# Gated linear attention, capacity routing and two expert layers on one core: attention matmuls grouped by tiling mode, weight conversion in place in one PSUM bank

## The chip, the cores and the metric

One core of one Trainium2 chip. The time is device microseconds (us) of one execution; less is better. A core has five engines that run beside each other: TensorE (PE, with its weight loads listed as PEld), VectorE (DVE), ScalarE (ACT), GpSimd (POOL) and SyncE (SP, which here issues DMA). Each takes its instructions in the order in which they were written.

## The reference, cut to what matters

```python
# attention: B, H, S, D = 4, 8, 768, 48
f = 1 / (1 + exp(-f_logit))
for t in range(S):
    state = f[:, :, t, :, None] * state + einsum('bhd,bhe->bhde', k[:, :, t], v[:, :, t])
    y[:, :, t] = einsum('bhd,bhde->bhe', q[:, :, t], state)
...
# x = y as (3072, 384); each of 8 experts takes at most 384 tokens, best logits first
h = maximum(x[mask] @ w1[e], 0); out[mask] = h @ w2[e]
...
# second layer for all tokens; w_in (384, 2048) and w_out (2048, 384) come as float64
h = x @ w_in
out = (h * cos(h)) @ w_out
```

## The kernel before, in words

The kernel has three stages: attention with the expert logits, a search for the first expert's tokens (`search`, `route`), and the experts with the cosine layer (`experts`). The change is in the first stage alone, which ends when the last logits are counted.

Attention runs in chunks of 128 tokens. A unit u is one chunk c of one batch b (c, b = divmod(u, 4), 24 units); p runs over four pairs of heads. Step i of the loop at the end of `attention` works on up to five units at once: loads of unit i+2; `forget` and `decay` of unit i (logs of the gates on ACT; their running sums A on PE); `scale` of unit i-1 (em, ep on ACT; kT, qT on POOL); `turn`, `scores` and `cut` of unit i-2 (k transposed; q times k into sc; masked by DVE into m); `mix` and `outer` of unit i-3 (y from the state and from m; kv as k times v); `carry`, `fade` and `gate` of unit i-4 (state plus kv on DVE, state times decay on POOL, the product xl that holds x and the logits on PE, copied by ACT into xx and summed by DVE into lg). After every fourth unit (every second at the end) `first_counts` picks each token's best expert on DVE (L189 to L196) and counts with a matmul (cn). All engines follow the order of this code, which `in_order` pins.

Beside this, the two matrices of the cosine layer are converted from float64 to a high and a low fp32r part by `resident_weights`: 28 pieces, 12 of w_in (128 x 512) and 16 of w_out (128 x 384). A piece takes an absolute value on ACT (`head`), four DVE operations on its bits, a copy to the high part on ACT, and a subtraction to the low part on DVE (`tail`). It is a generator, conv; `fill(n)` runs it to its n-th next stop. Before, a piece has seven stops, a step runs eight (fills of 3, 2 and 3) and the steps from 24 on run three more. The work tile `wv` lies in SBUF, two of them, and the absolute value of piece i+1 is issued ahead of piece i's DVE work; only the last value `w` lies in a PSUM bank.

An fp32 matmul stands in the trace as two passes, each with its own weight load. Tiling modes: A, xl, tk and the state part of y use all 128 rows and columns of the array; y from m and kv use 128 rows and 48 columns; sc uses 64 rows.

Of the kernel before, what the change touches and what calls it, by code (L numbers as in the profile page):

```python
# [9 lines left out]
F32 = mybir.dt.float32  # L10
F32R = mybir.dt.float32r
BF16 = mybir.dt.bfloat16
I32 = mybir.dt.int32
AF = mybir.ActivationFunctionType
ALU = mybir.AluOpType
# [4 lines left out]
P = 128  # L20
B, H, S, D = 4, 8, 768, 48
# [3 lines left out]
NP = H // 2  # L25
# [5 lines left out]
TINY = 2.0**-15  # L31
# [71 lines left out]
def resident_weights(nc, wp, stg, ps, win, wout):  # L103
    V = nc.vector
    R = {
        "ih": wp.tile([P, 3, F2], F32R, name="wih"), "il": wp.tile([P, 3, F2], F32R, name="wil"),
        "oh": wp.tile([P, 16, HD], F32R, name="woh"), "ol": wp.tile([P, 16, HD], F32R, name="wol"),
    }
    wide = win.dtype != F32
    parts = []  # L110
    for k in range(3):
        for j in range(4):
            s = slice(j * 512, (j + 1) * 512)
            parts.append((R["ih"][:, k, s], R["il"][:, k, s], win[k * P:(k + 1) * P, s], 512))
    for f in range(16):
        parts.append((R["oh"][:, f], R["ol"][:, f], wout[f * P:(f + 1) * P, :], HD))
    raw, mid, fin = {}, {}, {}

    def load(i):
        if i < len(parts):  # L120
            n = parts[i][3]
            if wide:
                raw[i] = stg.tile([P, n, 2], I32, name="wr", tag="wr", bufs=3)
                nc.sync.dma_start(raw[i].rearrange("p n w -> p (n w)"), parts[i][2].bitcast(I32))
            else:
                raw[i] = stg.tile([P, n], F32, name="wr", tag="wr", bufs=3)
                nc.sync.dma_start(raw[i], parts[i][2])

    def head(i):
        if wide and i < len(parts):  # L130
            mid[i] = stg.tile([P, parts[i][3]], I32, name="wv", tag="wv", bufs=2)
            nc.scalar.activation(mid[i].bitcast(F32), raw[i][:, :, 1].bitcast(F32), AF.Abs)

    def tail(i):
        if i >= 0:
            V.tensor_tensor(parts[i][1], fin.pop(i), parts[i][0].bitcast(F32), op=ALU.subtract)

    def run():
        load(0)
        load(1)  # L140
        yield
        head(0)
        yield
        for i, (hi_part, _, _, n) in enumerate(parts):
            load(i + 2)
            head(i + 1)
            yield
            if wide:
                v, lo, hi = mid.pop(i), raw[i][:, :, 0], raw[i][:, :, 1]
                V.tensor_scalar(v.bitcast(F32), v.bitcast(F32), TINY, None, op0=ALU.max)  # L150
                yield
                V.tensor_scalar(v, v, 5, 2, op0=ALU.logical_shift_left, op1=ALU.logical_shift_right)
                yield
                V.scalar_tensor_tensor(v, hi, -2**30, v, op0=ALU.bitwise_and, op1=ALU.bitwise_or)
                yield
                tail(i - 1)
                yield
                fin[i] = ps.tile([P, n], F32, name="w", tag="w")
                V.scalar_tensor_tensor(fin[i].bitcast(I32), lo, 29, v, op0=ALU.logical_shift_right, op1=ALU.bitwise_or)
                yield  # L160
            else:
                tail(i - 1)
                fin[i] = raw[i]
                yield
            del raw[i]
            nc.scalar.copy(hi_part, fin[i])
            yield
        yield
        tail(len(parts) - 1)
    return R, run()  # L170


# [46 lines left out]
def attention(tc, nc, ctx, K, qk, qkvf, xs, Z, G, wp, wg, win, wout, consts, late):  # L219
    V, SC, PE, GP = nc.vector, nc.scalar, nc.tensor, nc.gpsimd  # L220
    ap = ctx.enter_context(tc.tile_pool(name="at", bufs=1))
    wk = ctx.enter_context(tc.tile_pool(name="wk", bufs=2))
    ps = ctx.enter_context(tc.tile_pool(name="aps", bufs=1, space=PSUM))
# [8 lines left out]
    yps = ps.tile([P, NP, P], F32, name="y", tag="y")  # L232
# [5 lines left out]
    st = {}  # L238

    def load(u):  # L240
        if u < NU:
            c, b = divmod(u, B)
            x = ring[u % 3]
            vf = wk.tile([P, 2, HD], F32, name="vf", tag="vf", bufs=6)
            src = qkvf[b, c * P:(c + 1) * P, 2:4]
            if u == 0:
                nc.sync.dma_start(vf[:, 1], src[:, 1])
            else:
                nc.sync.dma_start(vf, src)
            for j in range(2):  # L250
                nc.sync.dma_start(x[64 * j:64 * j + D], qk[b, c, j])
            if u == 0:
                nc.sync.dma_start(vf[:, 0], src[:, 0])
            st[u] = dict(x=x, v=vf[:, 0].rearrange("t (h d) -> t h d", h=H), f=vf[:, 1])
# [46 lines left out]
    def mix(u):  # L301
        c, b = divmod(u, B)
        d = st[u]
        T, v = st_all[b], d["v"]
        y = yps
        for p in range(NP):
            if c > 0:
                PE.matmul(y[:, p], T[:, p], d["qT"][:, p], start=True, stop=False)
            for j in range(2):
                PE.matmul(y[64 * j:64 * j + D, p], v[:, 2 * p + j], d["sc"][j][:, p], start=(c == 0), stop=True)  # L310
        yT = d["yT"] = wk.tile([P, NP, P], F32, name="yT", tag="yT")
        SC.copy(yT, y)

    def outer(u):
        if u // B < NCH - 1:
# [25 lines left out]
    def gate(u):  # L341
        c, b = divmod(u, B)
        yT = st.pop(u)["yT"]
        xl = ps.tile([P, NP, 2 * D + E], F32, name="xl", tag="tr")
        for p in range(NP):
            PE.matmul(xl[:, p], yT[:, p], K["turn"][:, p], start=True, stop=True)
        xx = wk.tile([P, HD], F32, name="xx", tag="xx", bufs=3)


        def rows():  # L350
            SC.copy(xx.rearrange("t (p e) -> t p e", p=NP), xl[:, :, :2 * D])
            nc.sync.dma_start(xs[b * S + c * P:b * S + (c + 1) * P], xx)

        if u < NU - 1:
            rows()
        yield
        V.tensor_reduce(Z["lg"][:, u], xl[:, :, 2 * D:].rearrange("t p e -> t e p"), axis=AX, op=ALU.add)
        if u == NU - 1:
            rows()
        yield  # L360
        n = B if c < NCH - 1 else 2
        if b % n == n - 1:
            yield from first_counts(nc, wk, ps, K, Z, u - n + 1, n)

    def warm_up(n):
        w = ps.tile([P, 512], F32, name="wp", tag="kv")
        for _ in range(n):
            PE.matmul(w, warm[:, :P], warm, start=True, stop=True)

    def turning():  # L370
        K["turn"] = ap.tile([P, NP, 2 * D + E], F32, name="turn")
        V.memset(K["turn"], 0.0)
        for j in range(2):
            r = slice(64 * j, 64 * j + D)
            for p in range(NP):
                V.tensor_copy(K["turn"][r, p, D * j:D * j + D], K["ident"][r, r])
            nc.sync.dma_start(K["turn"][r, :, 2 * D:], wg.rearrange("(p j e) x -> j e p x", p=NP, j=2)[j])

    R, conv = resident_weights(nc, wp, wk, ps, win, wout)
    load(0)  # L380
    load(1)
    nc.sync.dma_start(K["wg"], wg.rearrange("(k p) e -> p k e", p=P))
    next(conv)
    gates = iter(())
    tail = late(ps)
    for i in range(NU + 5):
        def at(k, f, *a):
            if 0 <= i - k < NU:
                f(i - k, *a)

        def fill(n):
            for _ in range(n):
                next(conv, None)
        counts, gates = gates, gate(i - 4) if 0 <= i - 4 < NU else iter(())
        if i > NU:
            next(tail, None)
        at(4, carry)
        next(gates, None)
        at(2, turn)
        at(1, scale)  # L400
        F = (3, 2, 3) if i > 1 else (0, 0, 0)
        fill(F[0])
        at(3, mix)
        at(0, forget)
        next(counts, None)
        next(gates, None)
        fill(F[1])
        at(2, scores)
        fill(F[2])
        at(2, cut, 0)  # L410
        at(2, cut, 1)
        next(gates, None)
        at(4, fade)
        at(3, outer)
        at(0, decay)
        fill(0 if i < NU else 3)
        if i < len(WARM) and WARM[i]:
            warm_up(WARM[i])
        if i == 0:
            turning()  # L420
        load(i + 2)
# [436 lines left out]
def kernel(ctx, tc, qk, qkvf, wg, wcat, win, wout, out):  # L858
# [33 lines left out]
    with ExitStack() as actx:  # L892
        with in_order(tc, nc):
            R = attention(tc, nc, actx, K, qk, qkvf, xs, Z, G, wp, wg, win, wout, consts, late)
# [55 lines left out]
```

## Time and profile before

| what | value |
|---|---|
| median of 3 runs | 883.29 us (883.09 to 887.6) |
| the profiled execution: its time, its span | 883.84 us, 882.1 us |
| attention with its counts, from the span's start | to 188.8 us |
| PE, DVE, ACT, POOL busy over the span | 93%, 70%, 41%, 45% |
| mean granted TensorE clock | 0.977 of full speed |

The span is the time from the first to the last instruction; 1.74 us lie around it. A share of busy time is a mean over stages with different limits, so the prediction reads the first stage alone. Everything after 188.8 us follows in one chain that the change does not touch.

### The profile page before, as it was taken

To read this page: it belongs to the slowest core of one execution; us is meant where nothing else is said; L and a number is where in the kernel's file an instruction comes from. 1 tells how busy PE (TensorE), PEld (TensorE's weight loads), DVE (VectorE), ACT (ScalarE), POOL (GpSimd) and SP (SyncE) were. 2 spreads that over 40 slices of the span, in tenths; PEclk is the share of its full clock that TensorE was granted. 3 is DMA by queue.
4 is the path that set the end of the run, shared out by engine and by line. 5 is a ranking of instruction groups with operands and counts; after the bars stand their busy time and mean duration, and the time that the engine had idled before them with its cause. 6 is when DMAs were issued, how large, how long until landed. Compare 5 with 4: busy or idle time off the path is not lost.

```text
span 882.1 us, 15725 instructions
## 1 busy us (share of the span) xinstructions
PE 824.7 (93%) x5866; PEld 757.0 (86%) x5866; DVE 615.7 (70%) x1495; ACT 363.8 (41%) x686; POOL 393.5 (45%) x326
## 2 busy tenths in 40 slices
PE   6889999953999999999999999999999999999996
PEld 4767777642899989998999899899989999999996
DVE  6999999975679558846974696479557845652553
ACT  4866666511333523342344135323523352533332
POOL 4655555402514732572366047513731474734233
PEclk9999999975899999999999999999999999999999
DMA  9876756302302300230113012201400233300000
GB/s 238 254 230 185 228 184 211 97 29 84 90 1 70 102 27 1 81 110 8 54 46 100 1 55 81 63 1 59 113 28 1 81 99 99 87 3 28 1 1 27
DMA packets 27348, 71.90 MB, mean 82 GB/s; under 512 B 4608, under 2 KB 7936, under 8 KB 27264
## 3 DMA queue, kind: packets, MB, share of 16 engines
q1 hardware_dynamic: 24192, 61.38, 23.6%
q0 software_dynamic: 3072, 9.44, 3.3%
q8 instruction: 48, 0.79, 0.4%
q14 instruction: 36, 0.29, 0.1%
HBM read 61.37 MB, written 9.44 MB: 80 GB/s over the span
## 4 chain that ended last, share of the span: by engine, by line
PE 68%; DVE 6%; issue 1%; POOL 1%; DMA 1%; POOLq 0%; ACT 0%; DVEq 0%
PE pC L703 8%; PE accD L766 8%; PE pC L704 7%; PE accD L768 7%; PE pC L705 7%; PE accD L767 7%; PE pA L703 4%; PE pA L704 3%; PE accB L703 3%; PE pA L705 3%; PE accB L704 3%; PE accB L705 3%; DVE C L513 1%; PE cn L509 1%; DVE thr L561 1%; DVE thr L553 1%
## 5 line engine op out<-in xcount | busy, mean ns | idle before, releaser
L756 POOL TENSOR_TENSOR gl<-g,gh 128x384 fp32r<-128x384 f32 x128 | 134.6, 1052 | 266.0 <-ACT gh L755 262.3
L686 POOL TENSOR_TENSOR wl<-raw,wh 128x768 fp32r<-128x768 f32 x64 | 118.4, 1856 | 40.7 <-ACT wh L685 40.1
L766 PE MATMUL accD<-woh,gh 128*128 128x384 f32 x384 | 131.0, 341 | 0.0
L768 PE MATMUL accD<-woh,gl 128*128 128x384 f32 x384 | 130.3, 339 | 0.5 <-POOL gl L756 0.5
L705 PE MATMUL pC<-yTh,wil 128*128 128x384 f32 x384 | 130.2, 339 | 0.0
L767 PE MATMUL accD<-wol,gh 128*128 128x384 f32 x384 | 129.4, 337 | 0.0
L704 PE MATMUL pC<-yTl,wih 128*128 128x384 f32 x384 | 129.4, 337 | 0.0
L703 PE MATMUL pC<-yTh,wih 128*128 128x384 f32 x384 | 129.0, 338 | 0.0
L750 ACT ACTIVATE fr<-fr,halfpi 128x384 f32<-128x384 f32 x128 | 78.8, 616 | 105.0 <-DVE fr L749 97.1
L752 DVE TENSOR_TENSOR g<-pC,fr 128x384 f32<-128x384 f32 x128 | 71.0, 555 | 62.7 <-ACT fr L750 61.1
L755 ACT CAST gh<-g 128x384 fp32r<-128x384 f32 x128 | 65.7, 514 | 111.7 <-DVE g L752 98.5
L747 DVE TENSOR_SCALAR ki<-pC 128x384 int32<-128x384 f32 x128 | 70.9, 554 | 19.8 <-PE pC L705 18.8
L695 DVE SCALAR_TENSOR_TENSOR hl<-pA,hh 128x384 fp32r<-128x384 f32 x64 | 35.5, 555 | 66.9 <-ACT hh L694 66.7
L685 ACT CAST wh<-raw 128x768 fp32r<-128x768 f32 x64 | 52.7, 834 | 64.0 <-PE accB L704 32.8
L694 ACT ACTIVATE hh<-pA 128x384 fp32r<-128x384 f32 x64 | 31.5, 492 | 112.4 <-PE pA L705 112.4
L768 PEld LDWEIGHTS accD<-woh,gl 128*128 128x128 f32 x384 | 72.1, 188 | 1.6 <-POOL gl L756 1.1
L749 DVE SCALAR_TENSOR_TENSOR fr<-pC,ki 128x384 f32<-128x384 f32 x128 | 71.1, 556 | 3.1
L704 PEld LDWEIGHTS pC<-yTl,wih 128*128 128x128 f32 x384 | 72.1, 188 | 0.5 <-DVE yTl L698 0.5
L766 PEld LDWEIGHTS accD<-woh,gh 128*128 128x128 f32 x384 | 72.2, 188 | 0.1
L767 PEld LDWEIGHTS accD<-wol,gh 128*128 128x128 f32 x384 | 72.2, 188 | 0.0
L705 PEld LDWEIGHTS pC<-yTh,wil 128*128 128x128 f32 x384 | 72.1, 188 | 0.1
L703 PEld LDWEIGHTS pC<-yTh,wih 128*128 128x128 f32 x384 | 72.0, 188 | 0.1
(178 smaller groups left out, 1745.4 us busy)
## 6 DMA issues: line engine op xcount, KB each, us to landing
raw<-in_wcat_dram SPq DMA_DIRECT2D x64, 384.0 KB, 3.4
ring<-in_qk_dram SPq DMA_DIRECT2D x48, 192.0 KB, 4.9
vf<-in_qkvf_dram SPq DMA_DIRECT2D x23, 384.0 KB, 5.5
wr<-in_win_dram SPq DMA_DIRECT2D x12, 512.0 KB, 5.6
wr<-in_wout_dram SPq DMA_DIRECT2D x16, 384.0 KB, 3.2
xs<-xx SPq DMA_DIRECT2D x24, 192.0 KB, 2.4
vf<-in_qkvf_dram SPq DMA_DIRECT2D x2, 192.0 KB, 3.4
xg<-xs,idx POOLq DMA_INDIRECT x24, 3.1
```

Of the source, the lines that this page charges most:

```text
L686: GP.tensor_tensor(l, raw, h.bitcast(F32), op=ALU.subtract)
L703: PE.matmul(o, ah, bh, start=first, stop=False)
L704: PE.matmul(o, ah, bl, start=False, stop=False)
L705: PE.matmul(o, al, bh, start=False, stop=last)
L747: V.tensor_scalar(ki, p, INV2PI, 0.25, op0=ALU.mult, op1=ALU.add)
L749: V.scalar_tensor_tensor(fr, p, INV2PI, ki, op0=ALU.mult, op1=ALU.subtract)
L750: SC.activation(fr, fr, AF.Sin, bias=halfpi, scale=TWO_PI)
L752: V.tensor_tensor(g, p, fr, op=ALU.mult)
L756: GP.tensor_tensor(gl, g, gh.bitcast(F32), op=ALU.subtract)
L766: PE.matmul(r["accD"][t], gh[:, s], R["oh"][:, f], start=(f == 0), stop=False)
L767: PE.matmul(r["accD"][t], gh[:, s], R["ol"][:, f], start=False, stop=False)
L768: PE.matmul(r["accD"][t], gl[:, s], R["oh"][:, f], start=False, stop=(f == NF - 1))
```

## The change

In `resident_weights` the SBUF tile `wv` is gone. ACT writes the absolute value into the PSUM bank `w`, the four DVE operations work on it in place, ACT copies it to the high part, DVE subtracts. The next piece's absolute value has to wait for that subtraction, since there is one bank. A piece has four stops, a step runs four (one at each fill), and the steps from 24 on run three more.

In `attention` the state part of y is issued for all four pairs first and y from m after it, `outer` (kv) directly behind, then `scores`, then `decay`. On ACT `scale` comes first in a step and the copy of y (`settle`) last.

```diff
-    def head(i):
-        if wide and i < len(parts):
-            mid[i] = stg.tile([P, parts[i][3]], I32, name="wv", tag="wv", bufs=2)
-            nc.scalar.activation(mid[i].bitcast(F32), raw[i][:, :, 1].bitcast(F32), AF.Abs)
-
-    def tail(i):
-        if i >= 0:
-            V.tensor_tensor(parts[i][1], fin.pop(i), parts[i][0].bitcast(F32), op=ALU.subtract)
...
-        for i, (hi_part, _, _, n) in enumerate(parts):
+        for i, (hi_part, lo_part, _, n) in enumerate(parts):
             load(i + 2)
-            head(i + 1)
-            yield
             if wide:
-                v, lo, hi = mid.pop(i), raw[i][:, :, 0], raw[i][:, :, 1]
-                V.tensor_scalar(v.bitcast(F32), v.bitcast(F32), TINY, None, op0=ALU.max)
+                lo, hi = raw[i][:, :, 0], raw[i][:, :, 1]
+                w = ps.tile([P, n], F32, name="w", tag="w")
+                v = w.bitcast(I32)
+                nc.scalar.activation(w, hi.bitcast(F32), AF.Abs)
                 yield
+                V.tensor_scalar(w, w, TINY, None, op0=ALU.max)
                 V.tensor_scalar(v, v, 5, 2, op0=ALU.logical_shift_left, op1=ALU.logical_shift_right)
                 yield
                 V.scalar_tensor_tensor(v, hi, -2**30, v, op0=ALU.bitwise_and, op1=ALU.bitwise_or)
-                yield
-                tail(i - 1)
-                yield
-                fin[i] = ps.tile([P, n], F32, name="w", tag="w")
-                V.scalar_tensor_tensor(fin[i].bitcast(I32), lo, 29, v, op0=ALU.logical_shift_right, op1=ALU.bitwise_or)
-                yield
+                V.scalar_tensor_tensor(v, lo, 29, v, op0=ALU.logical_shift_right, op1=ALU.bitwise_or)
...
+            nc.scalar.copy(hi_part, w)
+            yield
+            V.tensor_tensor(lo_part, w, hi_part.bitcast(F32), op=ALU.subtract)
             del raw[i]
-            nc.scalar.copy(hi_part, fin[i])
             yield
...
+        for p in range(NP) if c > 0 else ():
+            PE.matmul(y[:, p], T[:, p], d["qT"][:, p], start=(p == 0), stop=False, skip_group_check=True)
         for p in range(NP):
-            if c > 0:
-                PE.matmul(y[:, p], T[:, p], d["qT"][:, p], start=True, stop=False)
             for j in range(2):
-                PE.matmul(y[64 * j:64 * j + D, p], v[:, 2 * p + j], d["sc"][j][:, p], start=(c == 0), stop=True)
-        yT = d["yT"] = wk.tile([P, NP, P], F32, name="yT", tag="yT")
-        SC.copy(yT, y)
+                PE.matmul(y[64 * j:64 * j + D, p], v[:, 2 * p + j], d["sc"][j][:, p], start=(c == 0 and p == 0), stop=True, skip_group_check=True)
+
+    def settle(u):
+        yT = st[u]["yT"] = wk.tile([P, NP, P], F32, name="yT", tag="yT")
+        SC.copy(yT, yps)
...
+        F = int(i > 1)
+        at(1, scale)
         at(4, carry)
+        fill(F)
         next(gates, None)
         at(2, turn)
-        at(1, scale)
-        F = (3, 2, 3) if i > 1 else (0, 0, 0)
-        fill(F[0])
+        next(counts, None)
         at(3, mix)
+        at(3, outer)
         at(0, forget)
-        next(counts, None)
+        fill(F)
         next(gates, None)
-        fill(F[1])
+        fill(F)
+        at(3, settle)
         at(2, scores)
-        fill(F[2])
+        next(gates, None)
+        at(4, fade)
+        at(0, decay)
+        fill(F)
         at(2, cut, 0)
         at(2, cut, 1)
-        next(gates, None)
-        at(4, fade)
-        at(3, outer)
-        at(0, decay)
         fill(0 if i < NU else 3)
```

On PE, one step of a unit with c > 0, before; a row counts matmuls (xN) before they are split into passes:

```order
L346 MATMUL xl<-turn,yT 128x104 x4
L283 MATMUL tk<-ident,kT 128x128 x4
L308 MATMUL y<-qT,st_139 128x128
L310 MATMUL y<-m,vf 48x128 x2
L308 MATMUL y<-qT,st_139 128x128
L310 MATMUL y<-m,vf 48x128 x2
...
L294 MATMUL sc_1244<-qT,kT 128x128
L294 MATMUL sc_1245<-qT,kT 128x128
...
L321 MATMUL kv<-vf,kk 48x48 x8
L264 MATMUL A<-mask,logs_93 128x128 x4
```

The same step of the changed kernel (L291 and L294 are now the two parts of y, L278 sc, L307 kv, L248 A):

```order
L332 MATMUL xl<-turn,yT 128x104 x4
L267 MATMUL tk<-ident,kT 128x128 x4
L291 MATMUL y<-qT,st_139 128x128 x4
L294 MATMUL y<-m,vf 48x128 x8
L307 MATMUL kv<-vf,kk 48x48 x8
L278 MATMUL sc_1224<-qT,kT 128x128
L278 MATMUL sc_1225<-qT,kT 128x128
...
L248 MATMUL A<-mask,logs_93 128x128 x4
```

The two parts of y no longer alternate, and kv moved ahead of sc.

On DVE, one settled step before, from the sum of the logits on (m is the cut, st the carry, the rest conversion):

```order
L357 TENSOR_REDUCE lg<-xl 128x8
L150 TENSOR_SCALAR wv<-wv 128x384
L152 TENSOR_SCALAR wv<-wv 128x384
L154 SCALAR_TENSOR_TENSOR wv<-wr,wv 128x384
L298 TENSOR_TENSOR m<-sc_1244,mask 128x512
L298 TENSOR_TENSOR m<-sc_1245,mask 128x512
L331 TENSOR_TENSOR st_139<-st_139,kv 48x4x48 x2
L136 TENSOR_TENSOR wol<-w,woh 128x384
L159 SCALAR_TENSOR_TENSOR w<-wr,wv 128x384
```

The same place of the changed kernel (L141 to L145 work on the PSUM bank, L151 is the subtraction, L282 the cut, L317 the carry):

```order
L343 TENSOR_REDUCE lg<-xl 128x8
L144 SCALAR_TENSOR_TENSOR w<-wr,w 128x512
L145 SCALAR_TENSOR_TENSOR w<-wr,w 128x512
L151 TENSOR_TENSOR wil<-w,wih 128x512
L282 TENSOR_TENSOR m<-sc_1224,mask 128x512
L282 TENSOR_TENSOR m<-sc_1225,mask 128x512
L317 TENSOR_TENSOR st_139<-st_139,kv 48x4x48 x2
L141 TENSOR_SCALAR w<-w 128x384
L142 TENSOR_SCALAR w<-w 128x384
```

The subtraction of a piece now stands directly behind its fourth DVE operation, with ACT's copy between the two.

On DVE at the end of the stage, before (the last subtraction, the last two units' logits, the count):

```order
L159 SCALAR_TENSOR_TENSOR w<-wr,wv 128x384
L887 CAST flag<-tot 1x1
L136 TENSOR_TENSOR wol<-w,woh 128x384
L215 TENSOR_TENSOR cn<-cn,cn_2333 128x8
L357 TENSOR_REDUCE lg<-xl 128x8
L889 TENSOR_LOAD flag
L357 TENSOR_REDUCE lg<-xl 128x8
L189 TENSOR_REDUCE mx<-lg 128x2
...
L196 TENSOR_TENSOR oh<-w,wm 128x16
L215 TENSOR_TENSOR cn<-cn,cn_2369 128x8
L524 TENSOR_SCALAR sat<-cn 128x8
```

The same place of the changed kernel:

```order
L145 SCALAR_TENSOR_TENSOR w<-wr,w 128x384
L151 TENSOR_TENSOR wol<-w,woh 128x384
L877 TENSOR_LOAD flag
L141 TENSOR_SCALAR w<-w 128x384
L142 TENSOR_SCALAR w<-w 128x384
L144 SCALAR_TENSOR_TENSOR w<-wr,w 128x384
L145 SCALAR_TENSOR_TENSOR w<-wr,w 128x384
L343 TENSOR_REDUCE lg<-xl 128x8
L151 TENSOR_TENSOR wol<-w,woh 128x384
L173 TENSOR_REDUCE mx<-lg 128x2
...
L199 TENSOR_TENSOR cn<-cn,cn_2341 128x8
```

The last piece is now converted between the last two sums of logits. After step 23 six pieces are still to be subtracted, where it was four.

## Rows read from the trace of the kernel before

**Rows 1.** Busy time by stretch: start:end, length, then busy us and instructions.

```profile
core 0: us, PE busy (x) PEld busy (x) DVE busy (x) ACT busy (x) POOL busy (x), PEclk, DMA share, GB/s
...
60.00:80.00 20.00, 19.66 (x205) 15.28 (x205) 19.49 (x33) 13.49 (x29) 10.95 (x8) 1.00 0.72 218
```

**Rows 2.** Timeline (start us, length us): A of units 2, 9, 13, 23; last count.

```profile
16.84 1.16 PE L264 MATMUL A<-mask,logs 128*128 128x128 f32 x8 [2.79 <-ACT logs L259]
...
66.82 1.16 PE L264 MATMUL A<-mask,logs 128*128 128x128 f32 x8 [0.17 <-ACT logs L259]
...
95.39 1.16 PE L264 MATMUL A<-mask,logs 128*128 128x128 f32 x8 [0.17 <-ACT logs L259]
...
167.59 1.16 PE L264 MATMUL A<-mask,logs 128*128 128x128 f32 x8 [0.66 <-ACT logs L259]
...
188.66 0.16 DVE L215 TENSOR_TENSOR cn<-cn,cn 128x8 f32<-128x8 f32 x1 [0.28 <-PE cn L211]
```

**Rows 3.** Timeline, weight loads of PE in one step; in brackets idle time before.

```profile
88.20 0.97 PEld L264 LDWEIGHTS A<-mask,logs 128*128 128x128 f32 x8
89.09 0.97 PEld L346 LDWEIGHTS xl<-turn,yT 128*128 128x128 f32 x8
89.96 0.47 PEld L283 LDWEIGHTS tk<-ident,kT 128*128 128x128 f32 x4
90.40 0.30 PEld L308 LDWEIGHTS y<-qT,st 128*128 128x128 f32 x2
...
92.02 0.30 PEld L308 LDWEIGHTS y<-qT,st 128*128 128x128 f32 x2 [0.18 <-issue]
...
92.79 0.30 PEld L308 LDWEIGHTS y<-qT,st 128*128 128x128 f32 x2 [0.18 <-issue]
...
93.57 0.97 PEld L294 LDWEIGHTS sc<-qT,kT 64*128 64x128 f32 x16 [0.18 <-issue]
94.66 0.44 PEld L321 LDWEIGHTS kv<-vf,kk 128*48 128x48 f32 x16
...
95.39 0.97 PEld L264 LDWEIGHTS A<-mask,logs 128*128 128x128 f32 x8 [0.29 <-ACT logs L259]
```

**Rows 4.** The same view in a step of a unit with c = 0.

```profile
27.26 0.82 PEld L310 LDWEIGHTS y<-m,vf 128*48 128x48 f32 x16 [0.17 <-issue]
...
28.27 0.97 PEld L294 LDWEIGHTS sc<-qT,kT 64*128 64x128 f32 x16 [0.19 <-issue]
```

**Rows 5.** Instructions by line: ns min/median/max, first and last start us, forms.

```profile
L150 DVE TENSOR_SCALAR wv<-wv x28: 348/1068/1504, 15.2 to 179.2; 128x384 f32<-128x384 f32 x16, 128x512 f32<-128x512 f32 x12
...
L154 DVE SCALAR_TENSOR_TENSOR wv<-wr,wv x28: 550/692/1644, 17.1 to 180.0; 128x384 int32<-128x384 int32 x16, 128x512 int32<-128x512 int32 x12
...
L136 DVE TENSOR_TENSOR wol<-w,woh x16: 544/550/559, 98.4 to 184.4; 128x384 fp32r<-128x384 f32 x16
L136 DVE TENSOR_TENSOR wil<-w,wih x12: 679/684/692, 21.2 to 92.1; 128x512 fp32r<-128x512 f32 x12
...
L747 DVE TENSOR_SCALAR ki<-pC x128: 542/555/560, 254.9 to 868.2; 128x384 int32<-128x384 f32 x128
...
L132 ACT ACTIVATE wv<-wr x28: 531/596/714, 14.5 to 175.9; 128x384 f32<-128x384 f32 x16, 128x512 f32<-128x512 f32 x12
...
L166 ACT CAST wih<-w x12: 566/586/617, 18.6 to 88.3; 128x512 fp32r<-128x512 f32 x12
```

**Rows 6.** Timeline of DVE and ACT: expert choice, cut and carry, the last piece.

```profile
81.97 0.17 DVE L189 TENSOR_REDUCE mx<-lg 128x4 f32<-128x32 f32 x1
...
83.33 0.19 DVE L196 TENSOR_TENSOR oh<-w,wm 128x32 bf16<-128x32 f32 x1
...
161.76 1.28 DVE L298 TENSOR_TENSOR m<-sc,mask 128x512 f32<-128x512 f32 x2
...
162.96 0.71 DVE L331 TENSOR_TENSOR st<-st,kv 48x192 f32<-48x192 f32 x2
...
183.86 0.48 ACT L166 CAST woh<-w 128x384 fp32r<-128x384 f32 x1 [3.64 <-DVE flag L887]
...
184.37 0.56 DVE L136 TENSOR_TENSOR wol<-w,woh 128x384 fp32r<-128x384 f32 x1 [0.50 <-ACT woh L166]
```

More of the change, by code (lines that the diff above doesn't have):

```diff
@@ L116, in resident_weights @@
         parts.append((R["oh"][:, f], R["ol"][:, f], wout[f * P:(f + 1) * P, :], HD))
-    raw, mid, fin = {}, {}, {}
+    raw = {}
     def load(i):
@@ L141, in run @@
         yield
-        head(0)
-        yield
-        for i, (hi_part, _, _, n) in enumerate(parts):
+        for i, (hi_part, lo_part, _, n) in enumerate(parts):
             load(i + 2)
-            head(i + 1)
-            yield
             if wide:
-                v, lo, hi = mid.pop(i), raw[i][:, :, 0], raw[i][:, :, 1]
-                V.tensor_scalar(v.bitcast(F32), v.bitcast(F32), TINY, None, op0=ALU.max)
+                lo, hi = raw[i][:, :, 0], raw[i][:, :, 1]
+                w = ps.tile([P, n], F32, name="w", tag="w")
+                v = w.bitcast(I32)
+                nc.scalar.activation(w, hi.bitcast(F32), AF.Abs)
                 yield
+                V.tensor_scalar(w, w, TINY, None, op0=ALU.max)
                 V.tensor_scalar(v, v, 5, 2, op0=ALU.logical_shift_left, op1=ALU.logical_shift_right)
@@ L154, in run @@
                 V.scalar_tensor_tensor(v, hi, -2**30, v, op0=ALU.bitwise_and, op1=ALU.bitwise_or)
+                V.scalar_tensor_tensor(v, lo, 29, v, op0=ALU.logical_shift_right, op1=ALU.bitwise_or)
+            else:
+                w = raw[i]
                 yield
-                tail(i - 1)
-                yield
-                fin[i] = ps.tile([P, n], F32, name="w", tag="w")
-                V.scalar_tensor_tensor(fin[i].bitcast(I32), lo, 29, v, op0=ALU.logical_shift_right, op1=ALU.bitwise_or)
-                yield
[L161 to L164, printed above, removed]
+            nc.scalar.copy(hi_part, w)
+            yield
+            V.tensor_tensor(lo_part, w, hi_part.bitcast(F32), op=ALU.subtract)
             del raw[i]
-            nc.scalar.copy(hi_part, fin[i])
             yield
-        yield
-        tail(len(parts) - 1)
     return R, run()
```

## The prediction

> **What bounds the kernel now.** I read the busy times by stretch first, since the change is in the first stage alone. There PE is busy 19.66 of 20 us and DVE 19.49 of 20, ScalarE 13.49, POOL 10.95 [rows 1]: two engines are full at once, and easing one of them alone would show the other. Then the starts of A, one in each step: from unit 2 to unit 23 they take 167.59 - 16.84 = 150.75 us, and the last 14 steps (100.77 us) 7.20 us each [rows 2]. The stage ends at 188.82 us with the last count, 21.23 us after A of unit 23 [rows 2]; the search and the experts follow it. What the stage gains or loses there, the kernel gains or loses.
>
> Next, what PE does in a step. From A to A it is 7.19 us: A 0.89, xl 0.87, tk 0.44, the two parts of y 3.17, sc 1.09, kv 0.44, and 0.29 of waiting for ACT's logs [rows 3]. In y the state part comes back every 0.77 us, and ahead of it the weight loads stand still for 0.18 us with nothing that the view could name [rows 3]. Where a unit has no state part, the sixteen passes from m follow each other in 0.82 us, with 0.17 to 0.19 us of standing still ahead of them and behind [rows 4]. So each change between the 128 x 128, the 48-column and the 64-row form costs about 0.19 us, and y alone has seven or eight of them.
>
> DVE looks full partly because its instructions are long. The first conversion operation (L150) takes 0.35 us at best and 1.07 in the median, L154 0.55 at best and up to 1.64; but the subtraction L136, which reads one operand from PSUM, never left 0.544 to 0.559 us (384 columns) and 0.679 to 0.692 (512) [rows 5]. What stretches the first two is absent where one operand is in PSUM.
>
> **The change part by part.** *PE.* Grouped, the state part costs what A's equal eight passes cost, 0.89, and y from m 0.82 [rows 3, 4]. A step then has three changes of form instead of ten. Sum: 0.89 (A) + 0.87 + 0.44 + 0.89 + 0.82 + 0.44 (kv) + 0.97 (sc) + 3 x 0.19 = 5.89 us. ACT issues the logs earlier than A needs them, since ScalarE no longer has the copy of y ahead of them, so the 0.29 goes too.
>
> *DVE.* The trace has no operation with both ends in PSUM. Lower bound: 0.35 us, the best of L150 [rows 5]; but ki (L747), the same kind of operation from PSUM, takes 0.555 for 384 columns, always. Upper bound: another 0.2 us on top, the 0.35 to 0.55 step being paid once for reading and once more for writing. I take what the one-PSUM rows show, 0.555 and 0.69, because L136, ki and the cut all give it whichever side is in PSUM.
>
> Against this part speaks a rule of the Trainium skill (VectorE: DVE Perf Modes, "Why PSUM operands drop a tier"): an fp32 operation with a PSUM operand loses the two-results-a-cycle mode. By it alone two operations of each piece go from 0.35 to 0.555 us, some 11 us more DVE work over 28 pieces; this trace has the 0.35 as L150's minimum but 1.07 as its median, by which the move gains. The skill's page SBUF — State Buffer ("Who interferes with whom") adds that a DVE instruction with at most one SBUF input outside that mode doesn't contend with GpSimd; by that, the trace agrees (L136 against L154).
>
> A step's loop on DVE, with a 512 piece: five operations 3.45; three gaps of 0.03 behind a dependent one 0.09; the trip to ScalarE for the high part 0.59 + 2 x 0.03 = 0.65 (183.86 to 184.37 is such a trip, 0.51 for 384 columns) [rows 5, 6]; carry 0.71; cuts 1.28; less three overlaps of 0.08 between independent neighbours, as between cut (to 163.04) and carry (from 162.96) [rows 6]. That is 5.95 us; with a 384 piece 2.78 + 0.09 + 0.54 + 0.71 + 1.28 - 0.24 = 5.16. The sum of the logits (0.18) fits into a gap. Every fourth step the expert choice adds 1.55 [rows 6] and a count 0.16, of which some 0.6 lies in the trip: +1.1, or 0.27 a step. So 6.2 us with a 512 piece (DVE is the bound) and 5.9 to 6.0 with a 384 piece (PE is, 5.43 against 5.89).
>
> *Steps.* From A of unit 2 to that of 13 are eleven steps with 512 pieces: 68.2 us, where it was 78.55 [rows 2]. To unit 23 ten with 384 pieces, 59.5, less 1.3 for the tk and kv that the last two lack: 58.2, where it was 72.20. Together 126.4 instead of 150.75: -24.4 us. The first four have no state part; I lay them out at 6 us, and the gain comes from the rest. Laid out the same way, the settled step before comes to 7.13 us, and the trace has 7.20; such odd waits, and DMA early in the stage, I charge with 2 us.
>
> *The end of the stage.* This is where it is given back. Before, four pieces were left after step 23, interleaved two deep; now six are, and each is one chain through one bank: ACT's absolute value 0.57 + 0.03, four DVE operations 4 x 0.555 + 0.09, the trip 0.54, the subtraction 0.555 + 0.03, together 4.04 us. Nothing of PE's is late enough to hide it. From A of unit 23: what DVE still has of that step (expert choice, subtraction, two cuts, a count) 3.4; six chains 24.2, less 0.6 for the first absolute value, which is hidden; cuts and one expert choice that don't fit into the trips 2.2; the last choice and count 1.8. That is 31.0 instead of 21.23: +9.8 us. The last sum of logits stands behind piece 28's four operations, so the search waits for all of them.
>
> *Free.* ScalarE's 13.49 and POOL's 10.95 us of 20 [rows 1] are 4.9 and 3.9 in a step of 7.2, so both still fit into 5.9; the loads, three buffers deep as before, are issued a step and more ahead. The copy of y now stands behind the high part on ScalarE; in steps that DVE bounds, xl waits for it by up to 0.7 us, which PE has to spare there, and without that slack it would cost as much a step. PE's longer idle time at the end may take its clock down some us earlier; xl of the last unit at half speed would be 1 us, beside DVE work.
>
> Sum: -24.4 + 2.0 + 9.8 = -12.6 us against the profiled execution's 883.84, so 871.2; the median of the runs shown lies 0.55 lower, hence **871 us**.
>
> **The rivals.** *In-place operations cost more than 0.555 and 0.69.* Five operations of twelve 512 pieces and six last pieces, 90 in all, lie on the path; 0.1 us more on each is 9 us, and about 1 more in the 384 steps, so 881. At 0.125 the gain is gone; from 0.16 the kernel is over 0.5% slower, and at 0.2 (the upper bound) 90 x 0.2 and 10 steps that outgrow PE by 0.5 give +23, so 894. This is the rival on the other side. For it: no row has both ends in PSUM; against it: one-sided rows are all alike.
>
> *Grouping doesn't lower the changes of form.* If the 0.77 us of a pair came from adding onto y, the settled step would stay at 7.15 and the first four at 6: 17 x 7.15 + 24 = 145.6, -5.2, with +9.8 at the end 888.5. Against it: the same 0.18 us stands ahead of sc, which adds nothing, and is missing among the sixteen passes that follow each other [rows 4].
>
> *The chains at the end are longer:* ScalarE's in-order copies in front of an absolute value, 1 us a piece, +6: 877.
>
> *More is gained:* DVE's overlaps are better and every step runs at PE's 5.89: 21 x 5.85 = 123, and no odd waits: 865.
>
> **How the numbers follow.** Main case 0.68 (866 to 877); dearer in-place operations 0.12 (877 to 888) and much dearer ones 0.06 (over 888); no grouping gain 0.05; longer chains 0.05; more gained 0.04. The likeliest gives 871. From 864 to 881 lie the main case, the gain, the longer chains and a third of the first rival, over 8 in 10. A measurement here can tell about 0.5%, 4.4 us, from no change. Faster by more than that (under 878.9): 0.68 + 0.05 + 0.04 and a third of 0.12, 0.81. Within it: 0.10. Slower: 0.09, from the much dearer operations and half of the no-grouping case.
>
> **What would show it.** Right: settled A to A 5.9 to 6.3 us instead of 7.2; 'issue' gaps of 0.18 only three to a step; L141 to L145 at 0.555 and 0.69 with hardly any spread; POOL's kT and qT with hardly any spread, too; A of unit 23 near 145 us; and from there to the last count about 31 us, DVE alternating with ScalarE. Wrong: in-place operations at 0.65 or more, steps still at 7 us, or DVE waiting elsewhere than for the high part and the absolute value. The search and all behind it should keep their lengths.

## The result and the profile after

The changed kernel takes 875.6 us (median of 4 runs, 875.32 to 876.22) beside 885.44 us for the kernel before on the same chip: a ratio of 0.989 (95% interval 0.9854 to 0.9926). Forecast were 871 us and a range of 864 to 881. The profiled execution's span is 874.0 us, where it was 882.1; the stage with attention ends at 180.23 us instead of 188.82, and what follows it keeps its length (693.8 and 693.3 us). So the 8 us are all in the stage, and two readings tell how: the steps became 18.4 us shorter and the end of the stage 9.5 us longer.

The timeline of the changed kernel, A of units 2, 3, 13 and 23 and the last count, beside [rows 2]:

```profile
17.08 1.71 PE L248 MATMUL A<-mask,logs 128*128 128x128 f32 x8 [2.08 <-ACT logs L243]
...
25.32 1.16 PE L248 MATMUL A<-mask,logs 128*128 128x128 f32 x8
...
89.48 1.16 PE L248 MATMUL A<-mask,logs 128*128 128x128 f32 x8
...
149.46 1.16 PE L248 MATMUL A<-mask,logs 128*128 128x128 f32 x8
...
180.07 0.16 DVE L199 TENSOR_TENSOR cn<-cn,cn 128x8 f32<-128x8 f32 x1 [0.28 <-PE cn L195]
```

From A of unit 2 to that of 23 it is 149.46 - 17.08 = 132.38 us (before 150.75; forecast 126.4 plus 2 of odd waits), from there to the last count 30.77 us (before 21.23; forecast 31.0). In the kernel before, A of unit 3, from which the table below counts, starts here:

```profile
24.86 1.16 PE L264 MATMUL A<-mask,logs 128*128 128x128 f32 x8 [1.24 <-ACT logs L259]
```

The weight loads of one step, beside [rows 3]:

```profile
108.74 0.97 PEld L248 LDWEIGHTS A<-mask,logs 128*128 128x128 f32 x8
...
110.94 0.97 PEld L291 LDWEIGHTS y<-qT,st 128*128 128x128 f32 x8
112.03 0.82 PEld L294 LDWEIGHTS y<-m,vf 128*48 128x48 f32 x16
112.83 0.51 PEld L307 LDWEIGHTS kv<-vf,kk 128*48 128x48 f32 x16
113.40 0.97 PEld L278 LDWEIGHTS sc<-qT,kT 64*128 64x128 f32 x16
114.49 0.97 PEld L248 LDWEIGHTS A<-mask,logs 128*128 128x128 f32 x8
```

The step is 5.75 us long and PE never waits in it. The two parts of y take 112.83 - 110.94 = 1.89 us, where they took 3.17 in four pieces of some 0.77 each.

The first in-place operation by line (ns min/median/max, first and last start, forms), beside [rows 5], and POOL's kT, in the changed kernel (L259) and in the one before (L275):

```profile
L141 DVE TENSOR_SCALAR w<-w x28: 555/567/700, 15.2 to 175.2; 128x384 f32<-128x384 f32 x16, 128x512 f32<-128x512 f32 x12
...
L259 POOL TENSOR_TENSOR kT<-ring,em x24: 1267/1280/1287, 7.3 to 151.4; 128x512 f32<-128x512 f32 x24
...
L275 POOL TENSOR_TENSOR kT<-ring,em x24: 1265/1282/1726, 7.4 to 170.7; 128x512 f32<-128x512 f32 x24
```

One value for each size, 0.56 and 0.70 us, with both ends in PSUM (L142 to L145 have medians of 563 to 567 ns and no more spread); the spread of 0.35 to 1.6 us is gone, and kT's (up to 1.73 us) with it.

Busy time from 60 to 80 us (the columns are those of [rows 1]), then a stretch of the end:

```profile
60.00:80.00 20.00, 17.96 (x228) 16.27 (x226) 17.98 (x37) 15.33 (x34) 11.76 (x11) 1.00 0.81 225
...
165.00:172.00 7.00, 3.60 (x26) 3.32 (x25) 5.36 (x13) 2.30 (x5) 0.00 (x0) 0.50 0.27 84
```

PE and DVE are no longer full: some 2 us of 20 are idle on each. A part of PE's idle time is a wait that the prediction didn't have; e5 below shows it. In the end PE's clock is down to half, as the prediction thought possible (before, it was 0.98 from 180 to 190 us).

### The profile page after: what moved, and what is told of

Read it like the earlier page. It is cut to its first block, busy times and chain, and to the rows that moved or that the text cites. A ratio compares the mean times of both kernels' runs of the same rounds, so it can differ in the third digit from the quotient of the medians.

```text
span 874.0 us, 15744 instructions
## 1 busy us (share of the span) xinstructions
PE 805.8 (92%) x5864; PEld 759.0 (87%) x5866; DVE 593.3 (68%) x1495; ACT 362.2 (41%) x686; POOL 382.5 (44%) x326
## 3 DMA queue, kind: packets, MB, share of 16 engines
q1 hardware_dynamic: 24192, 61.38, 25.1%
## 4 chain that ended last, share of the span: by engine, by line
PE 69%; DVE 6%; issue 1%; POOL 1%; DMA 0%; POOLq 0%; ACT 0%; DVEq 0%
PE pC L691 8%; PE accD L754 8%; PE pC L692 8%; PE accD L756 8%; PE pC L693 7%; PE accD L755 7%; PE pA L691 4%; PE pA L692 4%; PE accB L691 4%; PE pA L693 3%; PE accB L692 3%; PE accB L693 3%; DVE C L501 2%; PE cn L497 1%; DVE thr L549 1%; DVE thr L541 1%
```

## The experiments

The table gives, for each kernel, the time and what its trace shows of the stage: from A of unit 3 to A of unit 23 (the start of the stage is left out: kernels that are alike up to A of unit 3 reach it between 22.10 us, in e5, and 26.98 us, in e12, see the last section), and from there to the last count. The ratio is to the kernel before on the same chip; e5, e6, e7 and e12 can't be told apart by it, since their intervals overlap, and are told apart by their traces.

| kernel | median us | ratio (95% interval) | A of 3 to A of 23 | to the last count |
|---|---|---|---|---|
| before | 885.4 to 887.3 in four sets | 1 | 142.73 | 21.23 |
| changed | 875.6 | 0.989 (0.9854 to 0.9926) | 124.14 | 30.77 |
| changed, again (e11) | 874.43 | 0.9877 (0.9855 to 0.990) | 124.14 | 30.80 |
| e1, alternating y | 887.52 | 1.002 (1.0005 to 1.0035) | 135.11 | 31.27 |
| e2, work tile in SBUF | 889.99 | 1.0063 (1.0042 to 1.0085) | 138.65 | 30.75 |
| e3, conversion alone | 902.15 | 1.0192 (1.0157 to 1.0226) | 146.21 | 33.56 |
| e4, grouping alone | 881.6 | 0.9968 (0.9945 to 0.999) | 140.60 | 20.04 |
| e5, count in A's bank | 870.94 | 0.9832 (0.9811 to 0.9854) | 121.30 | 30.80 |
| e6, two banks at the end | 870.45 | 0.9825 (0.9803 to 0.9846) | 124.14 | 27.58 |
| e7, e5 and e6 | 869.72 | 0.9811 (0.9789 to 0.9833) | 121.16 | 27.66 |
| e8, exponentials and absolute value late | 911.4 | 1.0298 (1.0258 to 1.0338) | 159.58 | 33.01 |
| e9, exponentials late | 884.26 | 0.9985 (0.9964 to 1.0006) | 132.74 | 31.58 |
| e10, absolute value late | 889.51 | 1.004 (1.0022 to 1.0059) | 139.30 | 31.08 |
| e12, best version | 868.15 | 0.9804 (0.978 to 0.9827) | 121.15 | 25.12 |

**Is it the grouping? (e1)**

```diff
-        for p in range(NP) if c > 0 else ():
-            PE.matmul(y[:, p], T[:, p], d["qT"][:, p], start=(p == 0), stop=False, skip_group_check=True)
         for p in range(NP):
+            if c > 0:
+                PE.matmul(y[:, p], T[:, p], d["qT"][:, p], start=True, stop=False)
```

> The changed kernel with the two parts of y alternating again, pair by pair; conversion and all other orders as changed. Theory (each change of form costs about 0.19 us on PE): a step of a unit with a state part has ten changes of form again instead of three, 7 x 0.19 = 1.3 us; a 384 step goes from 5.75 to about 7.1 us, a 512 step from 6.15 to 7.1, the fourth steps (7.1 to 7.9) hardly change, so about +16 us: 891 (886 to 895). Rival (the conversion in place made the gain, DVE being the bound): PE has the slack, 876 (874 to 879).

It took 887.5 us, 12 to 13 more than the changed kernel: the theory holds, at a lower price than the 16 us expected. The weight loads of y in e1:

```profile
109.54 0.30 PEld L292 LDWEIGHTS y<-qT,st 128*128 128x128 f32 x2 [0.18 <-issue]
109.96 0.17 PEld L294 LDWEIGHTS y<-m,vf 128*48 128x48 f32 x4
110.31 0.30 PEld L292 LDWEIGHTS y<-qT,st 128*128 128x128 f32 x2 [0.18 <-issue]
```

The gap of 0.18 is back ahead of each state part, a pair takes 0.77 us again, and the step 6.75 us instead of 5.75. PE comes back to the state form three times more, which is six changes of form, so 1.00/6 = 0.17 us each. I had counted seven at 0.19; the seventh belongs to the place of kv, which in e1 still follows y from m.

**What does the PSUM bank give? (e2)**

```diff
-                w = ps.tile([P, n], F32, name="w", tag="w")
+                w = stg.tile([P, n], F32, name="w", tag="w", bufs=1)
```

> The changed kernel with the one work tile w in SBUF instead of in a PSUM bank, everything else the same. Theory (DVE's operations on SBUF alone are stretched while POOL works, those with a PSUM operand are not): the first two operations back to 0.35 at best and about 1 in the median, the next two up to 1.2 to 1.6, the subtraction stretched too, now that both its inputs are in SBUF; a 512 step +1 to +1.5 us, a 384 step +0.3 to +0.8; the end of the stage, where POOL rests, 2 us shorter: 888 (882 to 900). Rival (the PSUM rule alone: an fp32 operation with a PSUM operand is only slower): the first two take 0.35 and 0.4 instead of 0.56 and 0.70, so 868 (864 to 872).

It took 890.0 us, inside the theory's range. DVE and POOL side by side in e2, then one of the last pieces, where POOL has ended:

```profile
106.82 1.28 POOL L261 TENSOR_TENSOR qT<-ring,ep 128x512 f32<-128x512 f32 x1
106.96 1.35 DVE L141 TENSOR_SCALAR w<-w 128x384 f32<-128x384 f32 x1
108.05 1.06 POOL L325 TENSOR_TENSOR st<-st,G 128x448 f32<-128x448 f32 x1
108.35 0.97 DVE L142 TENSOR_SCALAR w<-w 128x384 int32<-128x384 int32 x1
109.46 0.55 DVE L144 SCALAR_TENSOR_TENSOR w<-wr,w 128x384 int32<-128x384 int32 x1
...
182.41 0.36 DVE L141 TENSOR_SCALAR w<-w 128x384 f32<-128x384 f32 x1 [0.61 <-ACT w L139]
```

L141 begins while POOL's qT runs and ends 0.21 us after it (108.31 and 108.10); L142 ends 0.21 us after POOL's next instruction (109.32 and 109.11); L144, with POOL at rest, takes its 0.55. L141 takes up to 1.53 us among the steps and 0.35 or 0.36 in the last five pieces. With 384 columns all 21 of L141 and L142 that run beside a POOL instruction end 0.21 to 0.23 us after one. So SBUF's price is a wait for the end of a POOL instruction rather than a slower rate. The Trainium skill (SBUF — State Buffer, "Who interferes with whom") says that GpSimd and a DVE instruction in a two-port mode share a pair of ports which the first to issue holds for its whole instruction, the other being blocked; by that, the trace agrees.

Three details came out otherwise. The subtraction, which met POOL only where it had started first, kept its 0.55 to 0.69 us. In two of the steps with 512 pieces PE's clock fell to half behind waits of 2.0 us for the copy of y (0.50 from 34.7 to 37.9 and from 48.3 to 51.6 us), which is a part of the loss. And the end of the stage is no shorter (30.75 us): the last four pieces follow each other in 3.7 us instead of 4.04, but DVE is already 1.1 us later against A of unit 23, and the first L141 behind it still meets POOL and takes 1.40.

**Does one part alone gain? (e3, e4)** e3 is the kernel before with the in-place conversion only (`resident_weights` as changed, fills of 1, 2 and 1), e4 the kernel before with the two loops of y only.

```diff
-        F = (3, 2, 3) if i > 1 else (0, 0, 0)
+        F = (1, 2, 1) if i > 1 else (0, 0, 0)
```

> The kernel before with the conversion in place in the one PSUM bank alone; matmul and ScalarE order as before, four stops a piece, fills of 1, 2 and 1. Theory (PE at 7.1 us a step is a bound of its own): settled steps 7.1 to 7.2, little less than before, and the end of the stage 8 to 10 us longer: 890 (884 to 896). Rival (DVE was the bound, so its shorter work is the gain): steps 6.2 to 6.4, 878 (873 to 882).

It took 902.2 us, above the expected range. PE did stay at 7.13 us in the settled steps, as the theory said, but every fourth step took 7.8 to 8.7 us and the end of the stage 33.6: 12 us dearer than I expected. In e3, as in e8 below, the exponentials and the absolute value stand behind `turn` on ScalarE; how much of the 12 us comes from it was not separated.

> The kernel before with the state part of y issued for all four pairs first and y from m behind it; nothing else changed. Theory (DVE, with its stretched operations on SBUF, is a bound of its own at about 7 us a step): PE's 1.3 us a step turn into waiting for DVE, settled steps 6.8 to 7.1: 880 (874 to 884). Rival (PE alone was the bound): steps 6.0, 861 (858 to 866).

It took 881.6 us, a gain of 0.3%, as the theory had it. From A of unit 13 on, with 384 pieces, the steps gained 5.1 us (67.06 instead of 72.20); from A of unit 3 to there, with 512 pieces, they lost 3.0 (73.54 instead of 70.53). One of its fourth steps took 11.1 us (80.25 to 91.36):

```profile
84.79 1.25 DVE L194 TENSOR_TENSOR w<-w,eb 128x32 f32<-128x32 f32 x1
...
87.95 0.27 PE L211 MATMUL cn<-oh,C 128*128 128x8 bf16 x4 [2.87 <-DVE st L331]
...
88.16 2.08 PE L294 MATMUL sc<-qT,kT 64*128 64x128 f32 x16
```

The expert choice falls beside POOL's kT and is stretched (L194 took 1.25 us; its like in the changed kernel, away from POOL, 0.18), the count matmul waits 2.87 us for the carry, and after that wait sc takes 2.08 us instead of 1.16: the granted clock is 0.50 from 87 to 92 us.

**Where did the forecast miss? (e5)**

```diff
-    cn = ps.tile([P, E], F32, name="cn0", tag="kv")
+    cn = ps.tile([P, E], F32, name="cn0", tag="A" if n == B else "kv")
```

> The changed kernel with the count matmul of the first two chunks in A's PSUM bank instead of kv's. Theory (in every fourth step that matmul waits for the bank until the carry, which stands behind the expert choice and two cuts on DVE, and PE's whole step waits with it): the four steps of 7.1 to 7.9 us fall to 6.5 to 7, -3 us: 872.5 (870 to 874). Rival (those steps are long because DVE has 1.7 us more in them, whoever waits): within 1 us of 875.6.

It took 870.9 us, and 2.8 us of the gain stand in the steps (124.14 to 121.30); the rest of the gain is in the start of the stage, which this edit doesn't touch. In the changed kernel the place that e5 mends reads so:

```profile
53.04 0.71 DVE L317 TENSOR_TENSOR st<-st,kv 48x192 f32<-48x192 f32 x2
...
53.80 0.26 PE L195 MATMUL cn<-oh,C 128*128 128x8 bf16 x4 [1.21 <-DVE st L317]
53.92 1.14 PE L291 MATMUL y<-qT,st 128*128 128x128 f32 x8
```

The count matmul writes the bank from which the carry (L317) reads kv; the carry stands behind the expert choice and two cuts; and y, kv, sc and A stand behind the count matmul. In e5 the wait is gone: the fourth steps with 384 pieces take 6.08 us instead of 7.15. With 512 pieces it is the rival that is nearer: the slow step and the one behind it together go from 13.51 to 13.16 us only. In e5's timeline DVE works through these two steps with no gap but the 0.65 us for the high part, so it is DVE that bounds them.

**What does the end cost? (e6, e7)** In e6 the last six pieces are two deep:

```diff
+            V.tensor_scalar(w, w, TINY, None, op0=ALU.max)
+            tail(i - 1)
+            head(i + 1)
+            V.tensor_scalar(v, v, 5, 2, op0=ALU.logical_shift_left, op1=ALU.logical_shift_right)
```

(`head` is the absolute value into the other bank, `tail` the subtraction.)

> The changed kernel with the last six pieces two deep: their work tiles alternate between the w bank and A's, which is free by then, the next absolute value is issued ahead, and the subtraction of a piece stands between the next piece's first two operations. Theory (a piece at the end costs its whole chain through one bank, 4.04 us, of which 1.1 are trips to ScalarE): 2.9 us a piece, the end of the stage 25 instead of 30.8 us: 870 (868 to 873). Rival (the end is set by the last units' products and logits on PE, whose clock is at half there): -1 us or nothing, 875 (873 to 877).

> The two together: count matmul of the first two chunks in A's bank, last six pieces two deep. If both stand, the gains add, as one lies in the steps and one behind them: 866.5 (863 to 870). If the end is then set by PE (half clock), only the first is left: 871 to 873.

e6 took 870.45 us with an end of 27.6 us instead of 30.8: 3.2 us of the 5.8 that I expected. That the median fell on the expected 870 all the same is luck, for the profiled execution took 872.16. The chain was what bounded the end at first, for with two banks DVE has no gap until 171.78 us; then it waits, and the rival is right about the rest:

```profile
167.92 0.20 PE L226 MATMUL cn<-oh,C 128*128 128x8 bf16 x2 [4.26 <-DVE flag L906]
167.97 2.06 PE L322 MATMUL y<-qT,st 128*128 128x128 f32 x8
...
174.72 0.19 DVE L374 TENSOR_REDUCE lg<-xl 128x8 f32<-128x32 f32 x1 [1.15 <-PE xl L363]
```

The product of the last unit stands behind a count matmul that waits 4.26 us for its bank, in which another small sum (tot, read into flag) still is; then it runs at half clock. e7 has the same end (27.7 us) and e5's steps (121.16), so both gains are in its trace; of its 869.7 us I expected 866.5, since I had counted on too much at the end.

**What is ScalarE's order worth? (e8, e9, e10)** e8 has `scale` and the fill that issues the next absolute value behind `turn`, as before; e9 moves `scale` alone, e10 the fill alone.

```diff
-        at(1, scale)
         at(4, carry)
-        fill(F)
         next(gates, None)
         at(2, turn)
+        at(1, scale)
+        fill(F)
```

> The changed kernel with the exponentials of A behind the copy of xl again on ScalarE (scale behind carry and turn, as before); nothing else changed. Theory (kT and qT have most of a step to spare, and PE does not wait for them): 876 (874 to 878). Rival (ScalarE's order is part of the gain: the exponentials wait for xl's product, POOL starts later, and A's bank comes free later): 0.2 to 0.5 us a step, 882 (879 to 887).

It took 911.4 us, 36 more than the changed kernel; both of my expectations were far off. Its waits from 60 to 150 us (us, times, longest):

```profile
...
DVE w L141 <- ACT w L139: 21.2, 11, 3.0
ACT xx L337 <- PE xl L332: 17.1, 11, 2.4
PEld xl L332 <- ACT yT L298: 15.4, 9, 2.2
...
ACT wih L149 <- DVE w L145: 12.3, 6, 2.1
```

In the changed kernel the first of them is 2.8 us in all and the third 2.2. Read as a ring they point to the cause: DVE waits for the absolute value, which stands on ScalarE behind the copy xx, which waits for xl on PE, which waits for the copy yT, which stands behind the high part, which waits for DVE's fourth operation. PE's clock adds to it: from 60 to 150 us the mean granted clock is 0.91, where the changed kernel has 1.00. From this I worked out e9 and e10.

> The changed kernel with the exponentials of A (scale) behind turn again on ScalarE, but the next piece's absolute value left where the change has it, ahead of the copy of xl. Theory (what the run with both moved showed is a loop through ScalarE: high part, copy of y, product xl, copies of xx and kk, exponentials, absolute value, then DVE's four operations; early absolute values break it, and kT and qT have time): 878 (874 to 884). Rival (the late exponentials themselves cost, through POOL's kT and A's bank): 895 or more.

> The changed kernel with the exponentials first, as changed, but the next piece's absolute value behind the copies of xx and kk. Theory (the loop without the exponentials: 0.59 high part + 0.59 copy of y + 1.2 xl + 0.48 xx + 0.59 kk + 0.7 absolute value + 0.3 + 2.8 on DVE = 7.2 us with a 512 piece, 6.5 with a 384 piece, instead of 6.15 and 5.75): 11 x 1.0 + 10 x 0.7 = +18, 893 (886 to 898). Rival (only the exponentials' place matters): 876 (874 to 879).

e10 (889.5 us) bears the ring out: with the absolute value late, the first 512 steps take 6.94 us (7.2 by the ring's sum) instead of 6.2, and the whole is 3.5 us below what I expected. Not all of its 15 us are the ring, though. Its two fourth steps with 512 pieces take 9.87 and 10.22 us (7.75 and 7.87 in the changed kernel): PE waits for the copy of y as well as for the carry, and then runs at half clock:

```profile
53.40 1.14 PE L332 MATMUL xl<-turn,yT 128*128 128x104 f32 x8 [0.91 <-ACT yT L298]
...
56.18 0.27 PE L195 MATMUL cn<-oh,C 128*128 128x8 bf16 x4 [1.21 <-DVE st L317]
56.31 2.05 PE L291 MATMUL y<-qT,st 128*128 128x128 f32 x8
```

e9 (884.3 us) lies between theory and rival. Its ordinary 384 steps are 5.75 us, as in the changed kernel, so late exponentials cost nothing there; its fourth steps take 10.0 us (A at 101.94 and 111.94):

```profile
101.10 1.27 POOL L261 TENSOR_TENSOR qT<-ring,ep 128x512 f32<-128x512 f32 x1
101.28 1.14 DVE L175 TENSOR_TENSOR w<-lg,mx 128x32 f32<-128x32 f32 x1
...
102.34 1.47 DVE L189 TENSOR_TENSOR C<-mx,t 128x512 bf16<-128x512 f32 x1
...
106.70 0.26 PE L195 MATMUL cn<-oh,C 128*128 128x8 bf16 x4 [2.29 <-DVE st L317]
106.82 1.74 PE L291 MATMUL y<-qT,st 128*128 128x128 f32 x8
```

It is what e4 showed: late exponentials put POOL's work beside the expert choice (L175 1.14 us; 0.19 in the changed kernel), the count matmul waits 2.29 us, and y then runs at the lower clock. The shares of the three were not separated. e9 and e10 cost 10 and 15 us beside e11, e8 36; so some 11 us appear only where both are late.

**The best version (e12)** has cn0 in A's bank throughout and the last six pieces two deep in SBUF:

```diff
+                two[i] = stg.tile([P, parts[i][3]], F32, name="w2", tag="w2", bufs=2)
...
+    cn = ps.tile([P, E], F32, name="cn0", tag="A")
```

> The changed kernel itself, on the same chip as the others of this set, to compare them with: 875.6 (874 to 877).

> Count matmul in A's bank throughout, and the last six pieces two deep in SBUF tiles instead of PSUM banks. Theory (DVE's operations on SBUF alone are stretched only while POOL works, and POOL has ended by then: 0.36 instead of 0.555 us for the first two of each; the last unit's product no longer stands behind a count matmul that waits for the bank of another small sum): 12 x 0.2 and 1.5 us less at the end than the run with both changes, 866 (863.5 to 868.5). Rival (the end is set by PE's products at half clock): 869 to 870.

868.15 us, at the upper edge of what I expected, beside 874.4 for the changed kernel on the same chip: 0.7% less. The end is 25.1 us, 2.5 less than in e7, where I had expected 3.9. PE's small count no longer waits, and L174 takes 0.35 us once POOL has ended:

```profile
162.63 0.19 PE L226 MATMUL cn<-oh,C 128*128 128x8 bf16 x2
...
164.88 0.35 DVE L174 TENSOR_SCALAR w<-w 128x384 f32<-128x384 f32 x1
```

## Why the prediction was right, and where it was off

The profiled execution lies some 4.5 us above the 871.2 of the sum: 4.0 in the steps, 0.2 ahead of A of unit 2, 0.4 behind the stage, and -0.2 in the end of the stage.

*PE's step.* Forecast 5.89 us, measured 5.75, where it was 7.19 [rows 3]. Right; e1 shows that 1.00 of the 1.44 us is the alternation in y, and the logs' wait of 0.29 is gone too. The sign of three gaps of 0.18 did not show as it was worded: behind the state part of y, kv and sc the weight loads pause for 0.06 to 0.12 us.

*In-place operations at 0.555 and 0.69.* Measured 0.56 and 0.70; the rival on the other side is refuted. e2 shows the reason that the prediction gave, one operand in PSUM keeping clear of POOL. The rule weighed against it (the Trainium skill, VectorE: DVE Perf Modes, "Why PSUM operands drop a tier") holds as well, 0.36 us in SBUF with POOL at rest beside 0.56 in PSUM, and e12 uses it where it pays, at the end.

*512 steps at 6.2.* Ordinary ones take 6.1 to 6.4 us. Right. The eleven steps at 68.2 us count all at 6.2, though; with the first four at 6, as the prediction says, they are 67.4.

*Every fourth step +1.1.* This is the term that failed, inside "Steps" with its 2 us for odd waits. The prediction counted the expert choice and the count as work of DVE and had no wait of PE for them. But the count matmul waits for the carry, whose bank it takes, so PE stands still by 1.0 to 1.4 us with half a step behind it: 7.75 and 7.87 us with 512 pieces, 7.15 with 384. With the count put elsewhere (e5) the steps sum to 2.8 us less, most of it with 384 pieces. The other part of the 4 us by which the steps are too long (132.4 against 128.4) is the first step: 8.24 us, where the repeated run has 6.58 and the prediction counted 6; PE was at half clock for a part of it (0.50 from 17.6 to 20.9 us). A of unit 23 stood at 149.46 us by these two, not near 145.

*The end of the stage.* Forecast 31.0, measured 30.77, and the mechanism is right: the last pieces follow each other in 4.04 and 4.05 us, where the sum has 4.04.

```profile
170.03 0.56 DVE L151 TENSOR_TENSOR wol<-w,woh 128x384 fp32r<-128x384 f32 x1 [0.48 <-ACT woh L149]
...
174.07 0.56 DVE L151 TENSOR_TENSOR wol<-w,woh 128x384 fp32r<-128x384 f32 x1 [0.55 <-ACT woh L149]
...
178.12 0.56 DVE L151 TENSOR_TENSOR wol<-w,woh 128x384 fp32r<-128x384 f32 x1 [0.45 <-ACT woh L149]
```

e6 and e12 show that it was the chain through one bank, with PE's late product behind it.

*Free.* The outcome was right, the argument was not enough. I weighed ScalarE by its busy time (4.9 us in a step of 5.9) and by the loads; e8 shows that with the same work a step takes 8.0 us in the mean, because one bank makes a ring of ScalarE, DVE and PE; PE's lower clock adds to it. The order of ScalarE, which I took as a thing that costs nothing, is what makes the other two parts a gain: with the exponentials and the absolute value late 911 us, with all three parts 875. Here the forecast was lucky, for nothing in its sums would have been different for e8. xl waits for the copy of y by up to 1.1 us (0.7 forecast).

*The rivals.* "Grouping doesn't lower the changes" is refuted by e1; "longer chains" by the end's 30.77; "more gained" needed steps at 5.85 throughout, and DVE holds the 512 steps at 6.2 and more even in e5.

## What to carry to other kernels

Where a bank is reused, read who reads it last and where that reader stands on its own engine: a matmul of 0.2 us held PE up for 1.2 us. A conversion through one buffer turns the engines' orders into a ring; write down what stands between two links of it on each engine before moving anything, since busy time doesn't show it. And parts of a change need not add: here the conversion alone lost 1.9%, the grouping alone gained 0.3%, both with ScalarE's exponentials and absolute value left late lost 3.0%, and the three together gained 1.1%.

## What the runs showed of the hardware that I had not expected

DVE on SBUF alone does not slow down beside POOL, it stops until POOL's instruction has ended (e2: DVE ends 0.21 to 0.23 us after POOL, 384 columns), and the reverse is there too: kT is 1.27 to 1.29 us in the changed kernel and up to 1.50 in e2.

PE's clock in the first 25 us differs between executions of one kernel. In the first profile of the changed kernel A of unit 2 took 1.71 us (the first timeline above); in the timeline of e11, the same kernel, it took 1.16, and the warm-up matmuls behind it 2.54 (3.49 in the first):

```profile
16.07 1.16 PE L248 MATMUL A<-mask,logs 128*128 128x128 f32 x8 [2.25 <-ACT logs L243]
17.29 2.54 PE L354 MATMUL wp<-warm 128*128 128x512 bf16 x11
```

From 16 to 25 us the granted clock is 0.81 in the first and 1.00 in the second, and the wait ahead of A is about the same, 2.08 and 2.25 us: a longer wait goes with the higher clock here. A of unit 3 starts at 25.32 and 22.65 us, and from there on the two agree to 0.03 us at the last count. Why, no run here tells.

After a wait of 2.3 to 2.9 us in the middle of the steps the clock is down to half (1.2 of 2.4 GHz) for some 3 to 7 us (e4: 0.50 from 87.0 to 93.7 us; e9: 0.50 from 107.3 to 110.5 us, y at 1.74 and 1.95 us instead of 1.06 and 1.08), and in e9 the two parts of y and kv behind the wait of 2.29 us take 1.7 us more. The length of the one wait doesn't tell whether the clock falls: behind waits of 1.0 to 1.2 us in the changed kernel's fourth steps y keeps its 1.14 and 1.08 us, while in e10, behind one of 1.21 us and one of 0.91 us ahead of xl, it takes 2.05 us.
